# A cross-attention and maxout kernel: a different order of work before and around the arrival of W1

## The chip, the cores and the metric

The kernel runs on one core of a Trainium2 chip. The metric is the device time of one execution in microseconds. Times are shown as the median of several runs; a profile is one further execution, recorded by the hardware profiler.

The core has five engines with instruction streams of their own: PE (TensorE: matmuls and transposes; its weight loads are shown apart, as PEld), DVE (VectorE), ACT (ScalarE), POOL (GpSimd) and SP (SyncE, which here only issues transfers). [...] Transfers between HBM and the on-chip memory run on 16 DMA engines.

## The reference, cut to what matters

```python
# x: (8, 8, 512, 64)  state: (8, 8, 32, 64)   batch, head, rows, width; all f32
scores = x @ state.T / 8;  a = softmax(scores);   xread = a @ state      # (8, 8, 512, 64)
scores2 = state @ x.T / 8; a2 = softmax(scores2); sread = a2 @ x         # (8, 8, 32, 64)
attn = concatenate([xread, sread], axis=2)        # 544 rows for each batch
X = attn.transpose(0, 2, 1, 3).reshape(4352, 512)
h1 = X @ w1; h2 = X @ w2                          # w1, w2: (512, 1024)
out = maximum(h1, h2) @ w_out                     # w_out: (1024, 512), out: (4352, 512)
```

## The kernel before, in words

**Algebra.** Since max(h1, h2) = h2 + relu(h1 - h2), the output is X·(W2·Wout) + relu(X·(W1 - W2))·Wout. The kernel keeps both factors side by side in one bf16 tile `wcat`: columns 0 to 1023 hold W1 - W2, columns 1024 to 1535 hold the product W2·Wout. Rows of X that come from xread are a·state, so the small state is multiplied with `wcat` first: `swt` = state·wcat (`u_sw`, products at L280), and then a·swt gives both h1 - h2 and the first term of the output. The softmax has no maximum subtracted.

**Per batch.** `compact_x` casts x to bf16 in its own layout (`xc`), `cast_x` casts it with a column of ones beside each 64 (`xp`). Transposed x (`xt`) comes from a DMA transpose of `xc` (`d_xt`), for batch 0 from TensorE transposes (`u_xt`). `u_exp` multiplies it with the block-diagonal state `sbd` (16 small matmuls in two groups, L216) and takes exp on ACT. `u_norm` sums, inverts and scales (DVE, and POOL or DVE) into `a`. `u_at` (or `d_at`, by DMA) transposes `a`. `u_sr` reads the state's rows back (32 small matmuls, L239, on `e` and `xp`), and `u_srt` transposes that into `sread_t`, which `moe_sread` uses at the very end. `l1` makes relu(a·swt) in eight column groups f of 128 (two matmuls each, L308, relu in turn on ACT and DVE, into `r`). `l2_open` starts four output banks with the first term (L319), `l2_add` adds r·Wout (L323), `l2_close` copies a bank out.

**Steady state.** For b = 1 to 7 the loop at L531 runs `l1(b)` and `l2(b)` and, in between, the pieces of batch b+1 and b+2 from `fillers`.

**The start.** All loads are issued by SP, on one queue, in the order of the code: state 0, x0 (two parts, even and odd heads), then for each half of W2 that half and two quarters of Wout, then the first half of W1 in two parts (called W1a here), the second half of W1 (W1b), x1, states 1 and 2, x2. `warm_up(n)` issues n matmuls on zeros, which nobody reads. While the weights arrive, PE transposes W2 (`w_t`, L401) and multiplies it with Wout (`w_wo` quarters 0 to 3, L412; `w_wo_out` copies the results into `wcat`). When W1a is in, it is cast (`w1b`), `u_sw(0, 0)` makes the first 512 columns of batch 0's `swt` straight from W1 and W2 (with `sneg`, the negated state), and `u_sw(0, 2)` the last 512. POOL then makes `wcat` columns 0 to 511 (`w_sub(0)`, `w_sub(1)`, L386), DVE makes 512 to 1023 (`w_sub(2)`, `w_sub(3)`) once W1b is in. `l1(0)` runs its first four f, then the second product's parts for these, and later the other four.

**What sets the order.** Every engine executes its instructions in the order of the code: the program is written out by hand, with `tc.manual_schedule()`, and the framework only adds the waits. PSUM has two pools of four banks: `ps` for short-lived results, `acc` for long sums. `xf_t` (f32 x) has two buffers, so x2 is loaded into the one of x0 once its casts are done, and x3 into that of x1.

Of the kernel before, what the change touches and what calls it, by code (L numbers as in the profile page):

```python
# [8 lines left out]
F32 = mybir.dt.float32  # L9
BF16 = mybir.dt.bfloat16  # L10
# [5 lines left out]
def kernel(  # L16
# [42 lines left out]
    def copy(eng, o, i):  # L59
        if eng == "A":  # L60
            nc.scalar.copy(o, i)  # L61
        elif eng == "V":
            nc.vector.tensor_copy(o, i)  # L63
        else:
            nc.gpsimd.tensor_copy(o, i)  # L65
# [11 lines left out]
    def load_x(b, parts=1):  # L77
        xf_t[b] = xio.tile([128, H, NC * D], F32, tag="xf", name="xf")
        for g in range(parts):
            nc.sync.dma_start(out=xf_t[b][:, g::parts, :], in_=x[b, g::parts].rearrange("h (p c) d -> p h (c d)", c=NC))  # L80
# [12 lines left out]
    def load_w(t, w, ch, parts=1):  # L93
        cs = slice(ch * 512, (ch + 1) * 512)
        for k in range(parts):
            i = slice(4 * k // parts, 4 * (k + 1) // parts)
            nc.sync.dma_start(out=t[:, i, cs], in_=w.rearrange("(i p) f -> p i f", p=128)[:, i, cs])  # L97
# [9 lines left out]
        load_wo(2 * ch)  # L107
        load_wo(2 * ch + 1)
    load_w(w1f, moe_w1, 0, 2)
    load_w(w1f, moe_w1, 1)  # L110
    load_x(1)
    load_states(second)
    load_x(2)

    ident = consts.tile([128, 128], BF16)
    warm = consts.tile([128, 512], BF16)
    nc.gpsimd.memset(warm, 0.0)  # L117
    make_identity(nc, ident)
    sbd = consts.tile([128, B, H, 2, Ns], BF16)
# [8 lines left out]
    def warm_up(n):  # L128
        p = bank()
        for k in range(n):  # L130
            nc.tensor.matmul(p, warm[:, 0:128], warm, start=(k == 0), stop=(k == n - 1))  # L131


    s_bf = stage.tile([128, 2 * B, 2, D], BF16)
# [25 lines left out]
    def negate_states():  # L160
        for g in range(2):
            gs = slice(64 * g, 64 * g + 64)
            negate("V", sneg[gs], sbd[gs, 0, g::2, g, :])
# [4 lines left out]
    st = {}  # L168
# [6 lines left out]
    def cast_x(b, parts=(("P", slice(0, 8)),)):  # L175
        new_x(b)
        xp = st[b]["xp"] = xio.tile([128, H, NC, 66], BF16, tag="xp", name="xp")
        nc.gpsimd.memset(xp[:, :, :, 64:65], 1.0)
        for e, hs in parts:
            copy(e, xp[:, hs, :, 0:64], xf_t[b][:, hs].rearrange("p h (c d) -> p h c d", c=NC))  # L180

    def compact_x(b, g, eng="A"):
        new_x(b)
        if g == 0:
            st[b]["xc"] = at.tile([128, H, NC * D], BF16, tag="xc", name="xc")
        copy(eng, st[b]["xc"][:, 4 * g:4 * g + 4], xf_t[b][:, 4 * g:4 * g + 4])


    def d_xt(b):
# [2 lines left out]
    def u_xt(b, g, eng):  # L192
        d = st[b]
        p = bank(BF16)
        for i in range(4):
            for c in range(NC):
                k = 2 * i + c // 2
                nc.tensor.transpose(p[64 * (c % 2):64 * (c % 2) + 64, k * 128:(k + 1) * 128], d["xp"][:, 2 * i + g, c, 0:64], ident)
        copy(eng, d["xt"].rearrange("p (i g u) t -> p g i (u t)", g=2, u=2)[:, g], p.rearrange("p (i w) -> p i w", i=4))

    def u_sc(b, g, mul=nc.gpsimd):
# [28 lines left out]
    def u_sr(b):  # L230

        d = st[b]
        d["sr"] = at.tile([128, 2, D], BF16, tag="sr", name="sr")
        d["rr"] = at.tile([128, 2], F32, tag="rr", name="rr")
        p = bank()
        for g in range(2):
            for c in range(NC):
                for i in range(4):
                    nc.tensor.matmul(p[32 * i:32 * i + 32, g * 65:g * 65 + 65], d["e"][:, g, i, c, :],  # L239
                                     d["xp"][:, 2 * i + g, c, 0:65],  # L240
                                     start=(c == 0 and g == 0), stop=(c == NC - 1 and g == 1))
        pv = p[:, 0:130].rearrange("p (g u) -> p g u", g=2)
        nc.vector.reciprocal(d["rr"], p[:, 64:130:65])
        nc.vector.tensor_mul(d["sr"], pv[:, :, 0:64], d["rr"].unsqueeze(2).to_broadcast([128, 2, D]))
# [173 lines left out]
    def fillers(b):  # L418
        fill = {}

        def put(slot, *units):
            fill.setdefault(slot, []).extend(units)

        n = b + 1
        if n < B:
            put(7, lambda: u_sc(n, 0), lambda: u_sc(n, 1))
            put(8, lambda: u_sr(n))
        if n + 1 < B:
            put(8, lambda: compact_x(n + 1, 0), lambda: compact_x(n + 1, 1))
        if n < B:  # L430
            put(9, lambda: d_at(n))
            put(10, lambda: u_sw(n, 0, 1, 2))
        if n + 1 < B:
            put(10, lambda: d_xt(n + 1))
        if n < B:
            put(11, lambda: u_srt(n))
        return fill

    for b in range(B):
        SW[b] = swt[:, b % 2]  # L440
    warm_up(6)
    cast_states("V", first)
    states(first)
    warm_up(9)
    cast_x(0, (("A", slice(0, 4, 2)), ("V", slice(4, 8, 2)), ("P", slice(1, 4, 2)), ("V", slice(5, 8, 2))))
    u_xt(0, 0, "V")
    warm_up(2)
    u_xt(0, 1, "A")
    u_exp(0, 0)
    warm_up(2)  # L450
    u_exp(0, 1)
    warm_up(3)
    w_cast(w2b, w2f, 0, "PA")
    u_norm(0, 0, nc.vector)
    u_norm(0, 1, nc.vector)
    w_t(0, 0, "A")
    w_t(0, 1, "A")
    u_sr(0)
    wo_cast(0, "P")
    wo_cast(1, "P")  # L460
    warm_up(1)
    for i in range(4):
        w_wo(0, i)
    u_at(0, "V")
    w_cast(w2b, w2f, 1)
    for i in range(4):
        w_wo(1, i)
    w_t(1, 0, "V")
    w_t(1, 1, "A")
    negate_states()  # L470
    wo_cast(2, "P")
    wo_cast(3, "P")
    u_srt(0)
    warm_up(2)
    for i in range(4):
        w_wo(2, i)
    for e, i in (("P", slice(0, 1)), ("A", slice(1, 2)), ("V", slice(2, 3)), ("A", slice(3, 4))):
# [7 lines left out]
    w_sub(0)  # L485
    w_sub(1)
    l1(0, {}, range(0, 4))
    w_sub(2, nc.vector)
    w_sub(3, nc.vector)
    compact_x(1, 0)  # L490
    compact_x(1, 1)
    d_xt(1)
    load_states(rest)
    cast_x(1, (("A", slice(0, 4)), ("A", slice(4, 8))))
    cast_states("P", second)
    compact_x(2, 0, "P")
    compact_x(2, 1, "P")
    d_xt(2)
    load_x(3)
    for c in range(NC):  # L500
        l2_open(0, c)
    l2_add(0, 0, range(0, 4))
    l2_add(0, 1, range(0, 4))
    states(second)
    l2_add(0, 2, range(0, 4))
    u_sw(0, 1)
    l2_add(0, 3, range(0, 4))
    l1(0, {}, range(4, 8))
    u_sw(1, 0)
    u_exp(1, 0)  # L510
    u_exp(1, 1)
    u_norm(1, 0, nc.gpsimd)
    u_norm(1, 1, nc.gpsimd)
    cast_states("P", rest)
# [58 lines left out]
```

The softmax here doesn't subtract the row's maximum and nothing guards it: scores larger than these inputs give would overflow.

## Time and profile before

| what | value |
|---|---|
| median of 8 runs | 150.0 us (149.46 to 151.0) |
| the profiled execution, its own time | 150.05 us |
| its span in the profile | 148.3 us |
| PE busy | 140.2 us, 95% |
| DVE, ACT, POOL busy | 81.2, 75.7, 44.3 us |
| moved by DMA | 29.89 MB, of it 0.16 MB in 10 packets on the queue "instruction" q8 |
| PE busy from 0 to 24.27 us | 20.97 us |
| PE busy from 24.27 to 40.34 us | 15.79 us |
| PE busy from 40.34 to 54.30 us | 13.86 us |

The span is the time from the first to the last instruction; the run's own time is 1.75 us longer. Busy time of PE has modelled ends. A row of a group or of the timeline gives line, engine, operation, output and inputs, shapes and count, and in brackets how long the engine sat idle before and what ended that. In the chain in order of time a row gives start, length, and what the time was spent on. `l1(0)` begins at 24.27 us, `l1(1)` at 40.34 us, `l1(2)` at 54.31 us.

### The profile page before, as it was taken

How to read it: one execution, taken by the hardware profiler on the slowest of the kernel's cores; microseconds unless marked ns; L12 is line 12 of the kernel's file. 1: busy time of each engine (PE TensorE's matmuls, PEld its weight loads, DVE VectorE, ACT ScalarE, POOL GpSimd, SP SyncE). 2: the span in 40 equal slices, each digit the busy share in tenths (PEclk: the TensorE clock that was granted, in tenths of full speed). 3: DMA queues.
4: the chain of work that ended last, by engine and by line, in shares of the span. 5: the costliest groups of instructions: out<-in, count | busy, mean ns of one | idle time of the engine just before them, and what ended most of it. 6: DMA issues, size and time to landing. Idle time of an engine off the chain costs nothing.

```text
span 148.3 us, 3003 instructions
## 1 busy us (share of the span) xinstructions
PE 140.2 (95%) x1228; PEld 67.7 (46%) x1249; DVE 81.2 (55%) x150; ACT 75.7 (51%) x127; POOL 44.3 (30%) x48
## 2 busy tenths in 40 slices
PE   6988989999999999999999999999999999999991
PEld 2455633344454445434543454454445434764460
DVE  5338538848787187535835581668067625721130
ACT  3157348687477177546844692487167036521011
POOL 3145169651949310650072027004100500000000
PEclk9999999999999999999999999999999999999999
DMA  2999999879999949893979497760566031502423
GB/s 74 374 390 386 387 383 339 270 132 212 240 206 380 287 80 288 280 185 102 288 238 186 155 285 197 146 272 13 101 116 283 0 75 46 236 0 70 139 91 131
DMA packets 37982, 29.89 MB, mean 202 GB/s; under 512 B 24912, under 2 KB 33360, under 8 KB 37072
## 3 DMA queue, kind: packets, MB, share of 16 engines
q1 hardware_dynamic: 37824, 29.56, 69.1%
q8 instruction: 10, 0.16, 0.4%
q10 hardware_dynamic: 144, 0.13, 0.3%
q14 instruction: 4, 0.03, 0.1%
HBM read 15.20 MB, written 8.91 MB: 163 GB/s over the span
## 4 chain that ended last, share of the span: by engine, by line
PE 76%; SPq 9%; DMA 9%; issue 2%; POOL 1%; DVE 0%; ACT 0%
PE acc L323 35%; PE ps L308 18%; DMA s_f<-in_state_dram 9%; PE acc L319 8%; SPq L97 4%; PE ps L280 3%; SPq L80 3%; PE ps L367 2%; PE acc L377 2%; PE ps L216 2%; SPq L100 2%; PE ps L239 2%; PE acc L357 1%; PE acc L375 1%; POOL s_bf L65 1%
## 5 line engine op out<-in xcount | busy, mean ns | idle before, releaser
L323 PE MATMUL acc<-wo,r 128*128 128x512 bf16 x238 | 58.3, 379 | 0.5
L323 PEld LDWEIGHTS <-r 128*128 128x128 bf16 x248 | 23.9, 98 | 28.3 <-issue 0.2
L298 DVE TENSOR_SCALAR r<-ps 128x512 bf16<-128x512 f32 x32 | 22.1, 691 | 13.6 <-PE ps L308 13.6
L226 POOL TENSOR_TENSOR a<-e,er 128x512 bf16<-128x512 bf16 x14 | 14.4, 1048 | 50.4 <-ACT e L219 29.7
L308 PE MATMUL ps<-aT,swt 128*128 128x512 bf16 x127 | 29.1, 380 | 0.3 <-DVE swt L63 0.2
L63 DVE COPY ob<-acc 128x512 f32<-128x512 f32 (+1 forms) x17 | 11.1, 655 | 30.2 <-PE acc L323 29.8
L61 ACT COPY ob<-acc 128x512 f32<-128x512 f32 (+1 forms) x16 | 9.2, 572 | 28.9 <-PE acc L323 13.1
L296 ACT ACTIVATE r<-ps 128x512 bf16<-128x512 f32 x32 | 19.2, 601 | 5.9 <-PE ps L308 5.3
L308 PEld LDWEIGHTS <-swt 128*128 128x128 bf16 x128 | 12.1, 98 | 14.9 <-DVE swt L63 0.8
L319 PE MATMUL acc<-swt,aT 128*128 128x512 bf16 x56 | 16.7, 381 | 0.8 <-issue 0.8
L61 ACT CAST swt<-ps 128x512 bf16<-128x512 f32 x18 | 9.9, 587 | 13.1 <-PE ps L280 13.0
L65 POOL CAST xp<-xf 128x2048 bf16<-128x2048 f32 (+1 forms) x7 | 12.2, 1743 | 11.6 <-DMA xf<-in_x_dram 11.6
L61 ACT CAST xc<-xf 128x1024 bf16<-128x1024 f32 x12 | 12.0, 1050 | 1.4 <-DMA xf<-in_x_dram 1.4
L223 DVE TENSOR_REDUCE es<-e 128x16 f32<-128x512 bf16 x16 | 10.6, 660 | 3.6 <-ACT e L219 3.6
L63 DVE CAST swt<-ps 128x512 bf16<-128x512 f32 x18 | 11.6, 678 | 1.1 <-PE ps L280 1.1
L131 PE MATMUL ps<-warm 128*128 128x512 bf16 x24 | 8.7, 498 | 1.3 <-POOL warm L117 1.3
L219 ACT ACTIVATE e<-ps 128x512 bf16<-128x512 f32 x16 | 8.8, 596 | 0.8
L412 PE MATMUL acc<-wo,w2t 128*128 128x512 bf16 x30 | 7.3, 379 | 0.6 <-POOL wo L65 0.5
L319 PEld LDWEIGHTS <-aT 128*128 128x128 bf16 x62 | 4.7, 98 | 6.0 <-issue 2.5
L280 PE MATMUL ps<-wcat,sbd 64*32 64x512 bf16 x136 | 6.2, 383 | 0.0
L216 PEld LDWEIGHTS <-xt 128*128 128x128 bf16 x128 | 4.8, 98 | 2.8 <-ACT xt L61 0.8
L216 PE MATMUL ps<-sbd,xt 128*128 128x64 bf16 x128 | 5.4, 193 | 0.6 <-ACT xt L61 0.6
(74 smaller groups left out, 118.0 us busy)
## 6 DMA issues: line engine op xcount, KB each, us to landing
xf<-in_x_dram SPq DMA_DIRECT2D x7, 1024.0 KB, 7.5
out_dram<-ob SPq DMA_DIRECT2D x7, 1024.0 KB, 5.0
w2f<-in_moe_w_dram SPq DMA_DIRECT2D x2, 1024.0 KB, 9.2
wof<-in_moe_w_out_dram SPq DMA_DIRECT2D x4, 512.0 KB, 11.1
xf<-in_x_dram SPq DMA_DIRECT2D x2, 512.0 KB, 4.6
w1f<-in_moe_w_dram SPq DMA_DIRECT2D x2, 512.0 KB, 13.5
w1f<-in_moe_w_dram SPq DMA_DIRECT2D x1, 1024.0 KB, 14.3
out_dram<-ob SPq DMA_DIRECT2D x3, 256.0 KB, 2.1
```

The lines of the kernel that those rows point to most:

```text
L61: nc.scalar.copy(o, i)
L63: nc.vector.tensor_copy(o, i)
L65: nc.gpsimd.tensor_copy(o, i)
L216: nc.tensor.matmul(p[:, k * 64:k * 64 + 64], d["xt"][:, 4 * i + 2 * g + cp, :], sbd[:, b, 2 * i + g].rearrange("p u n -> p (u n)"), start= ...
L223: nc.vector.tensor_reduce(d["es"][:, g], d["e"][:, g].rearrange("p i c n -> p (i c) n"), axis=mybir.AxisListType.X, op=ALU.add)
L226: mul.tensor_mul(d["a"][:, g].rearrange("p c i n -> p i c n"), d["e"][:, g], d["er"][:, g].rearrange("p (i c) -> p i c", i=4).unsqueeze(3) ...
L280: nc.tensor.matmul(pg[g][32 * i:32 * i + 32, :], sneg[gs, i, :] if k else sbd[gs, b, 2 * i + g, g, :], w[gs, i, ch * 512:(ch + 1) * 512], ...
L296: nc.scalar.activation(out=o, in_=p, func=ACTF.Relu)
L298: nc.vector.tensor_scalar(o, p, scalar1=0.0, scalar2=None, op0=ALU.max)
L308: nc.tensor.matmul(p, SW[b][:, g, f * 128:(f + 1) * 128], AT[b][:, g, :], start=(g == 0), stop=(g == 1))
L319: nc.tensor.matmul(OB[b][1 + c], AT[b][:, g, c * 128:(c + 1) * 128], SW[b][:, g, FF:WC], start=(g == 0), stop=False)
L323: nc.tensor.matmul(OB[b][1 + c], R[b][:, f, c * 128:(c + 1) * 128], wo[:, f, :], start=False, stop=(f == NF - 1))
```

## The change

It reorders the start and makes some of its TensorE work with other instructions:

- x1 and states 1 and 2 are loaded before W1b instead of after it.
- The tile of the warm-ups is f32, 128x256, instead of bf16, 128x512. There are 8 warm-up matmuls (2, 5 and 1) instead of 25 (6, 9, 2, 2, 3, 1 and 2).
- Batch 0's x is transposed from `xc`, 128 columns at a time, in 16 transposes instead of 32 of 64 columns from `xp`. `compact_x` takes its parts as an argument. `xp` of batch 0 is cast later, on ACT, in two copies.
- `negate_states` goes from after `w_t(1)` to before batch 0's casts. The second part of the first half of W2 is cast on DVE instead of ACT.
- `u_sr(0)` and `u_srt(0)` go from before W1 to after `states(second)` and after the second half of `l1(0)`.
- After the first half of `l1(0)`: `w_sub(2)` and `w_sub(3)` come after `states(second)` and `u_sr(0)` on DVE; `states(second)` comes right after `l2_open`, ahead of all `l2_add`; `compact_x(2)` comes later; all four `l2_add(0, c, 0..3)` come before `u_sw(0, 1)`; `u_sw(1, 0)` comes before the second half of `l1(0)`, and `u_exp(1)` inside it, after f = 5.

```diff
     load_w(w1f, moe_w1, 0, 2)
-    load_w(w1f, moe_w1, 1)
     load_x(1)
     load_states(second)
+    load_w(w1f, moe_w1, 1)
     load_x(2)
...
-    warm = consts.tile([128, 512], BF16)
+    warm = consts.tile([128, 256], F32)
...
-            nc.tensor.matmul(p, warm[:, 0:128], warm, start=(k == 0), stop=(k == n - 1))
+            nc.tensor.matmul(p[:, 0:256], warm[:, 0:128], warm, start=(k == 0), stop=(k == n - 1))
...
-    def compact_x(b, g, eng="A"):
+    def compact_x(b, parts=(("A", slice(0, 4)), ("A", slice(4, 8)))):
         new_x(b)
-        if g == 0:
-            st[b]["xc"] = at.tile([128, H, NC * D], BF16, tag="xc", name="xc")
-        copy(eng, st[b]["xc"][:, 4 * g:4 * g + 4], xf_t[b][:, 4 * g:4 * g + 4])
+        xc = st[b]["xc"] = at.tile([128, H, NC * D], BF16, tag="xc", name="xc")
+        for e, hs in parts:
+            copy(e, xc[:, hs], xf_t[b][:, hs])
...
         for i in range(4):
-            for c in range(NC):
-                k = 2 * i + c // 2
-                nc.tensor.transpose(p[64 * (c % 2):64 * (c % 2) + 64, k * 128:(k + 1) * 128], d["xp"][:, 2 * i + g, c, 0:64], ident)
+            for cp in range(2):
+                k = 2 * i + cp
+                nc.tensor.transpose(p[:, k * 128:(k + 1) * 128], d["xc"][:, 2 * i + g, cp * 128:(cp + 1) * 128], ident)
...
-    warm_up(6)
+    warm_up(2)
     cast_states("V", first)
     states(first)
-    warm_up(9)
-    cast_x(0, (("A", slice(0, 4, 2)), ("V", slice(4, 8, 2)), ("P", slice(1, 4, 2)), ("V", slice(5, 8, 2))))
+    warm_up(5)
+    negate_states()
+    compact_x(0, (("A", slice(0, 4, 2)), ("V", slice(4, 8, 2)), ("P", slice(1, 4, 2)), ("V", slice(5, 8, 2))))
     u_xt(0, 0, "V")
-    warm_up(2)
     u_xt(0, 1, "A")
     u_exp(0, 0)
-    warm_up(2)
     u_exp(0, 1)
-    warm_up(3)
-    w_cast(w2b, w2f, 0, "PA")
+    warm_up(1)
+    w_cast(w2b, w2f, 0, "PV")
...
-    u_sr(0)
     wo_cast(0, "P")
     wo_cast(1, "P")
-    warm_up(1)
...
     w_cast(w2b, w2f, 1)
+    cast_x(0, (("A", slice(0, 4)),))
     for i in range(4):
         w_wo(1, i)
     w_t(1, 0, "V")
     w_t(1, 1, "A")
-    negate_states()
+    copy("A", st[0]["xp"][:, 4:8, :, 0:64], xf_t[0][:, 4:8].rearrange("p h (c d) -> p h c d", c=NC))
     wo_cast(2, "P")
     wo_cast(3, "P")
-    u_srt(0)
-    warm_up(2)
     for i in range(4):
         w_wo(2, i)
...
     l1(0, {}, range(0, 4))
-    w_sub(2, nc.vector)
-    w_sub(3, nc.vector)
-    compact_x(1, 0)
-    compact_x(1, 1)
+    compact_x(1)
     d_xt(1)
     load_states(rest)
     cast_x(1, (("A", slice(0, 4)), ("A", slice(4, 8))))
     cast_states("P", second)
-    compact_x(2, 0, "P")
-    compact_x(2, 1, "P")
+    for c in range(NC):
+        l2_open(0, c)
+    states(second)
+    u_sr(0)
+    w_sub(2, nc.vector)
+    w_sub(3, nc.vector)
+    l2_add(0, 0, range(0, 4))
+    l2_add(0, 1, range(0, 4))
+    compact_x(2, (("P", slice(0, 4)), ("P", slice(4, 8))))
     d_xt(2)
     load_x(3)
-    for c in range(NC):
-        l2_open(0, c)
-    l2_add(0, 0, range(0, 4))
-    l2_add(0, 1, range(0, 4))
-    states(second)
     l2_add(0, 2, range(0, 4))
+    l2_add(0, 3, range(0, 4))
     u_sw(0, 1)
-    l2_add(0, 3, range(0, 4))
-    l1(0, {}, range(4, 8))
     u_sw(1, 0)
-    u_exp(1, 0)
-    u_exp(1, 1)
+    l1(0, {5: [lambda: u_exp(1, 0), lambda: u_exp(1, 1)]}, range(4, 8))
+    u_srt(0)
```

## The prediction

> **What bounds the kernel now.** I read the page first: PE is busy 95% of the span. That is an average over a start that waits for weights and a rest that doesn't, so the next view is the chain of work that ended last, in order of time.
>
> ```profile
> PE 140.2 (95%) x1228; PEld 67.7 (46%) x1249; DVE 81.2 (55%) x150; ACT 75.7 (51%) x127; POOL 44.3 (30%) x48
> ...
> q8 instruction: 10, 0.16, 0.4%
> ```
> ```profile
> 14.97 13.33 DMA s_f<-in_state_dram
> 28.35 1.29 POOL s_bf L65
> 29.69 0.40 PE ps L155 x4
> ...
> 40.40 3.57 PE ps L308 x16
> ```
>
> Up to 28.30 us the chain is the load queue: the states of batches 1 and 2 land, POOL casts them, PE transposes them at 29.69. Afterwards it is PE nearly alone; from 40.34 (start of `l1(1)`) each batch takes 13.97 us. The change touches nothing behind that point, so the question is when `l1(1)` starts. The timeline shows what leads there:
>
> ```profile
> 18.12 2.23 POOL L65 CAST wo<-wof 128x1024 bf16<-128x1024 f32 x2 [4.63 <-DMA wof<-in_moe_w_out_dram]
> ...
> 19.21 3.61 PE L412 MATMUL acc<-wo,w2t 128*128 128x512 bf16 x15 [0.54 <-POOL wo L65]
> ...
> 21.99 0.43 DVE L63 CAST w1b<-w1f 128x512 bf16<-128x512 f32 x1 [2.58 <-DMA w1f<-in_moe_w_dram]
> ...
> 22.04 4.91 POOL L386 TENSOR_TENSOR wcat<-w1f,w2f 128x1024 bf16<-128x1024 f32 x2 [0.77 <-DMA w1f<-in_moe_w_dram]
> ...
> 24.27 1.90 PE L308 MATMUL ps<-aT,swt 128*128 128x512 bf16 x8 [0.21 <-DVE swt L63]
> ...
> 30.88 0.41 PE L280 MATMUL ps<-wcat,sbd 64*32 64x512 bf16 x8
> ...
> 31.36 0.69 DVE L63 CAST swt<-ps 128x512 bf16<-128x512 f32 x1 [0.37 <-PE ps L280]
> ```
>
> Before 24.27 every engine waits for a landing: Wout's third quarter (POOL, 18.12), then W1a's second part (DVE, 21.99). From 24.27 PE has next to no gap. So PE work taken out ahead of W1 is worth nothing by itself; PE work put behind 24.27 costs its full time.
>
> But landings are not set by bytes alone. The list of DMA issues, asked in short windows, gives the four Wout quarters in turn, an instruction packet at 15.87, and W1a's second part (issued 9.07):
>
> ```profile
> wof<-in_moe_w_out_dram SPq DMA_DIRECT2D x1, 512.0 KB, 8.1
> ...
> wof<-in_moe_w_out_dram SPq DMA_DIRECT2D x1, 512.0 KB, 8.9
> ...
> wof<-in_moe_w_out_dram SPq DMA_DIRECT2D x1, 512.0 KB, 13.6
> ...
> q8 instruction: 1, 0.02, 68.8%
> ...
> w1f<-in_moe_w_dram SPq DMA_DIRECT2D x1, 512.0 KB, 12.9
> ```
>
> Quarters 0 and 1 (issued 2.85 and 3.40) land at 10.96 and 12.31, 1.35 us apart. W2's second half lands at 15.03; quarter 2 (issued 4.43) should follow at 16.4 and lands at 18.07. Semaphore times show that 15 of 16 DMA engines had delivered it by 16.38 and one came at 18.07; the same engine stays behind to the end (W1a: 15 engines by 20.43, the last 21.97). The step of 1.55 to 1.7 us coincides with that 16 KB packet of PE instructions, 15.87 to 16.97. Without it W1a lands at 20.43.
>
> [...] ten packets of 16 KB for some 2,500 weight loads and matmuls; four of the five packets from the fourth to the eighth began when 256·k minus 62 to 68 of them had started. [...]
>
> **The change, part by part.** (1) *PE ahead of W1.* 25 warm-ups, 16 transposes, `u_sr(0)` and `u_srt(0)` go, 8 f32 warm-ups come. Time: nothing, as said; the cover is the wait for the weights. If that were gone it would be 8.7 us of warm-ups less 8 f32 ones[...]. Count: up to quarter 1's product today 290 instructions (two per matmul), afterwards 148 plus those of the f32 matmuls: 16 if each is one pair, 32 if two, 64 if four. [...] Today that is 12.6 us, and the packet comes 3.2 us later[...]. Afterwards it is the same count: within `w_t(1)`, near 17.0, with 16; at the end of quarter 1's product, near 16.5, with 32; near 15 with 64. With the same 3.2 us the packet starts at 20.2, 19.7 or 18. To spare W1a it must start after 20.4. I take 19.7: W1a lands late, at 21.97, while quarters 2 and 3 land early.
>
> (2) *ACT and DVE ahead of W1.* ACT gets two casts of 1.0 us for `xp`, loses a `w2b` cast (1.04) and `sread_t` (0.27); it sits idle 2.12 and 1.23 us there today. DVE gets a 0.68 us cast before 10.5, where it is idle 1.96. `negate_states` (1.03) delays an x cast that the warm-ups cover until 7. Nothing. SP issues the same 1024 KB and 128 KB in another order; x2 now also waits for ACT's late `xp` casts, near 20, while SP reaches it at 21.
>
> (3) *Start of `l1(0)`.* With W1a at 21.97 DVE's w1b cast, two `wcat` casts and `swt` follow as now: 24.2.
>
> (4) *States earlier in PE's order.* `states(second)` now stands before all `l2_add`. Its cast is on POOL behind both L386 (22.04 to 26.95), a memset (to 27.14) and 1.28 us: 28.42, although the states land by 25.6. PE gets there at 24.2 + 1.73 + 1.73 = 27.7 and stands until 28.47, S. Behind it on PE queue `u_sr(0)`, the 16 `l2_add` and all that follows.
>
> (5) *From S to `u_sw(1, 1)`*, today 29.69 to 35.97, 6.28 us. Afterwards: transposes 0.24; `u_sr(0)` 0.47 with its switch; 16 `l2_add` at 0.216, 3.46; 0.1 for DVE, which ends `sbd` copies, `sr` and two `w_sub` at S + 1.8 + 2.43; then `u_sw(0, 1)` to `l1`, 1.22, as today from 30.88 to 32.10, but filled by 0.34 of `u_sw(1, 0)` where 0.86 of `l2_add` stood; f = 4, 5 0.86; `u_exp(1)` 0.47; f = 6, 7 0.86; `u_srt` 0.06; then `l2_add` needs f = 7, whose relu follows f = 6's on DVE and ACT, ACT having two exps of 0.55 in between: 0.35; four `l2_add` 0.86. Sum 8.95. Of x1's gain (`xt` earlier) nothing is left: PE waited under 0.2 for it.
>
> (6) The rest to `l1(1)` has the same order: 35.97 to 40.34, 4.37.
>
> Sum: 28.47 + 8.95 + 4.37 = 41.79 against 40.34, +1.45 us. The span becomes 149.75, the run 150.05 + 1.45 = 151.5; the profiled run stands 0.05 over the median, so the median as well.
>
> **Rivals.** *The packet comes after 20.4* (not slower). W1a lands at 20.43: L386 runs 20.5 to 25.4; x1 and the states land by 25.6 (the late engine is late for them instead), cast until 26.9, S = 26.95. `l1(0)` starts near 22.8. S + 13.32 = 40.27: 150.0. For it: one pair for an f32 matmul, or a slower fetch, moves the packet by the missing 0.2 to 0.7. Against: 3.2 us is already the longest delay of the ten, counted so; the others are 0.6 to 2.7. It decides at a start of 20.4.
>
> *PE loses its clock.* Today warm-ups start 0.427 us apart until 6.2 us and 0.216 after. With fewer of them between 7 and 12 the products before 16 could run at half speed; quarters 0 and 1 cost 3.4 us more, `l1(0)` starts 1 to 2 us later: 152.5 to 153.5. [...]
>
> *The waits of (4) and (5) are smaller*, with an early W1a: without the 0.8 at S and half of the others, 149.0. For it: POOL's two L386 differ (2.36, 2.60). Against: their chain from W1a to S has no slack anywhere.
>
> *No effect of instruction packets at all*: then 151.5 too.
>
> **How the numbers follow.** Forecast, with the last rival: 0.52, 150.9 to 152.2 by its waits. Packet late: 0.34, 149.5 to 150.8. Clock: 0.08. Smaller waits: 0.06. A measurement of this kernel tells 0.3%, 0.45 us, from no change. Faster: 0.06 and 0.08 out of the second case, 0.14. Same: 0.20 of the second and 0.02 of the first, 0.22. Slower: 0.50, 0.06 and 0.08, 0.64. The range 149.6 to 152.3 leaves out about 0.1 at each end.
>
> **What would show it.** Right: an instruction packet between 17.5 and 20.4, W1a's second cast near 22.0, POOL's state cast ending at 28.4, PE standing 0.7 to 0.8 before L155, a gap of 0.5 between L280 and L308 near 33. Wrong: no such packet before 20.4, and w1b cast at 20.5; or L155 reached by PE later than the cast, which makes POOL harmless; or f32 warm-ups that keep PE beyond 8 us.

## The result, and the profile after

The kernel after takes 150.58 us (median; 150.2 to 150.9), the kernel before, on the same chip, 149.84. The ratio is 1.0044, with a 95% interval from 1.0031 to 1.0057: slower by 0.66 us (0.46 to 0.85). The forecast was 151.5. It had the sign, and the time lies in its range, but it had worked out a loss of 1.45 us, 0.8 us too much. The profiled execution took 150.71 us, its span is 148.9 us.

The page first, its line of busy time and the queue of PE instructions:

```profile
PE 139.5 (94%) x1204; PEld 69.6 (47%) x1224; DVE 81.6 (55%) x151; ACT 76.6 (51%) x128; POOL 44.4 (30%) x48
...
q8 instruction: 9, 0.15, 0.4%
```

PE is 0.7 us less busy in a span that is some 0.7 us longer. Half of the idle time that this adds lies ahead of W1, where the warm-ups went (busy 20.20 of 24.20 us instead of 20.97 of 24.27) and where it costs nothing. One instruction packet fewer came. The chain of work that ended last, in order of time (start, length, what), shows where it is decided now:

```profile
9.13 12.77 DMA w1f<-in_moe_w_dram
...
24.20 1.90 PE ps L308 x8
26.10 1.73 PE acc L319 x8
27.82 0.22 PE ps L155 x4
28.05 0.37 PE ps L239 x32
...
32.39 0.69 DVE swt L63
...
41.07 0.97 PE ps L308 x4
```

Before, the chain was the load queue up to 28.30 us: the states. Now the load of W1a ends in it at 21.90, and from 24.20 it is PE without a step of POOL: L155, the transposes of the states, follows L319 directly. Between there and `l1(1)` the only pieces of another engine are DVE's cast of `swt` at 32.39 and one relu (0.70 us at 34.20). The timeline of each engine has the same places (start, length, engine, line, operation; in brackets the idle time before and what ended it):

```profile
21.97 4.91 POOL L386 TENSOR_TENSOR wcat<-w1f,w2f 128x1024 bf16<-128x1024 f32 x2 [0.76 <-DMA w1f<-in_moe_w_dram]
...
24.20 1.90 PE L308 MATMUL ps<-aT,swt 128*128 128x512 bf16 x8 [0.21 <-DVE swt L63]
...
26.89 0.61 POOL L65 CAST s_bf<-s_f 128x512 bf16<-128x512 f32 x1
...
27.66 0.39 PE L155 MATMUL ps<-ident,s_bf 128*128 128x128 bf16 x4
27.98 0.44 PE L239 MATMUL ps<-xp,e 128*32 128x65 bf16 x32
...
33.13 1.04 PE L308 MATMUL ps<-aT,swt 128*128 128x512 bf16 x4 [0.59 <-DVE swt L63]
...
36.64 0.41 PE L280 MATMUL ps<-wcat,sbd 64*32 64x512 bf16 x8
...
41.00 1.25 PE L308 MATMUL ps<-aT,swt 128*128 128x512 bf16 x5
```

Three things are to be seen. POOL's state cast takes 0.61 us, not the 1.28 of the forecast, and ends at 27.49, before PE wants it: PE starts L155 at 27.66 with no wait. The forecast had named this among its signs of being wrong (L155 reached by PE later than the cast ends). From there everything stands where the forecast put it, 0.8 us earlier: `u_sw(1, 1)` 8.98 us after S (forecast 8.95), `l1(1)` another 4.36 us later (4.37), the gap before f = 4 at 33.13. And `l1(0)` starts at 24.20 as forecast, since W1a is late as before.

The list of DMA issues and queues, asked for 18 to 19.5 us, has the packet of PE instructions that the forecast placed at 19.7, 3.2 us after the start of PE's 180th instruction (that it follows the 180th was the author's assumption); it starts at 18.17:

```profile
q8 instruction: 1, 0.02, 4.7%
```

**Where the 0.66 us come from.** From the start of `l1(0)` to that of `l1(1)` PE takes 16.80 us instead of 16.07; `l1(0)` itself starts 0.07 earlier. Of these 0.73 us, 0.53 are `u_sr(0)` and `u_srt(0)` (0.47 and 0.06), which stand behind W1 now. The rest, 0.20, is a balance of waits: PE now stands 0.59 us before f = 4, to 33.13, and short waits of the kernel before, at L155 and around `u_exp(1)` (L216), are gone. No run takes this balance apart.

### The profile page after: what moved, and what is told of

Read it like the earlier page. It is cut to its first block, busy times and chain, and to the rows that moved or that the text cites. A ratio compares the mean times of both kernels' runs of the same rounds, so it can differ in the third digit from the quotient of the medians.

```text
span 148.9 us, 2957 instructions
## 1 busy us (share of the span) xinstructions
PE 139.5 (94%) x1204; PEld 69.6 (47%) x1224; DVE 81.6 (55%) x151; ACT 76.6 (51%) x128; POOL 44.4 (30%) x48
## 4 chain that ended last, share of the span: by engine, by line
PE 80%; DMA 9%; SPq 5%; DVE 2%; issue 2%; ACT 0%
PE acc L323 36%; PE ps L308 19%; PE acc L319 9%; DMA w1f<-in_moe_w_dram 9%; PE ps L280 3%; SPq L97 2%; PE ps L367 2%; PE acc L377 2%; PE ps L239 2%; SPq L100 2%; PE ps L216 2%; PE acc L357 1%; PE acc L375 1%; DVE swt L63 1%; PE acc L280 1%
## 5 line engine op out<-in xcount | busy, mean ns | idle before, releaser
L308 PE MATMUL ps<-aT,swt 128*128 128x512 bf16 x126 | 29.2, 380 | 1.0 <-DVE swt L63 0.8
L308 PEld LDWEIGHTS <-swt 128*128 128x128 bf16 x128 | 11.9, 98 | 15.5 <-DVE swt L63 1.6
L319 PE MATMUL acc<-swt,aT 128*128 128x512 bf16 x56 | 16.7, 381 | 0.8 <-issue 0.8
L65 POOL CAST xp<-xf 128x2048 bf16<-128x2048 f32 x6 | 11.3, 1890 | 10.6 <-DMA xf<-in_x_dram 10.6
L61 ACT CAST xc<-xf 128x1024 bf16<-128x1024 f32 (+1 forms) x13 | 12.6, 1017 | 3.5 <-DMA xf<-in_x_dram 3.5
L131 PE MATMUL ps<-warm 128*128 128x256 f32 x16 | 7.0, 603 | 1.1 <-POOL warm L117 1.1
L319 PEld LDWEIGHTS <-aT 128*128 128x128 bf16 x62 | 4.7, 98 | 5.9 <-issue 2.5
L280 PE MATMUL ps<-wcat,sbd 64*32 64x512 bf16 x136 | 6.0, 382 | 0.1
L65 POOL CAST xc<-xf 128x1024 bf16<-128x1024 f32 (+1 forms) x3 | 3.3, 1123 | 9.1 <-DMA xf<-in_x_dram 9.1
L216 PEld LDWEIGHTS <-xt 128*128 128x128 bf16 x128 | 4.8, 98 | 2.6 <-DVE xt L63 0.5
```

What stands on the lines that cost most here:

```text
L280: nc.tensor.matmul(pg[g][32 * i:32 * i + 32, :], sneg[gs, i, :] if k else sbd[gs, b, 2 * i + g, g, :], w[gs, i, ch * 512:(ch + 1) * 512], ...
L308: nc.tensor.matmul(p, SW[b][:, g, f * 128:(f + 1) * 128], AT[b][:, g, :], start=(g == 0), stop=(g == 1))
L319: nc.tensor.matmul(OB[b][1 + c], AT[b][:, g, c * 128:(c + 1) * 128], SW[b][:, g, FF:WC], start=(g == 0), stop=False)
```

## The experiments

Three questions: what each part of the change costs, why the cast took half of its price, and what the instruction packet does to the loads. Kernels that ran together share the runs of the kernel before: d1 to d4, d5 to e2, e3 to f3, g2 to g4, and h1 with h2 (its medians are 149.79, 149.76, 149.81, 149.76 and 149.74 us). "W1a" is the landing of its second part on the 15th and on the last of the 16 DMA engines, S the start of L155. These columns are from one profiled execution each, the medians are not. In each of the 18 profiles of this table the execution's own time is 109.70 to 109.74 us more than its `l1(1)`: nothing behind that point makes a difference, as the forecast took it, and what a kernel gains or loses can be read from that column. (d1 is not in the table; its profile is described below.)

| kernel | median, us | ratio to before, 95% | packet | W1a | `l1(0)` | S | `l1(1)` |
|---|---|---|---|---|---|---|---|
| before (first profile) | | | 15.87 | 20.43, 21.97 | 24.27 | 29.69 | 40.34 |
| after (first profile) | | | 18.17 | 20.48, 21.90 | 24.20 | 27.66 | 41.00 |
| d2 | 152.22 | 1.013 to 1.019 | 20.77 | 20.28, 20.42 | 24.99 | 28.45 | 42.52 |
| d3 | 150.34 | 1.0022 to 1.0047 | 18.12 | 20.47, 21.43 | 23.73 | 27.20 | 40.36 |
| d4 | 149.84 | 0.9987 to 1.0015 | 15.77 | 20.54, 21.38 | 23.68 | 28.87 | 39.86 |
| d5 | 150.92 | 1.0058 to 1.0132 | 18.11 | 20.32, 21.57 | 23.87 | 27.63 | 40.98 |
| d6 (after again) | 150.76 | 1.0041 to 1.0080 | 18.17 | 20.41, 22.15 | 24.45 | 27.91 | 41.26 |
| e1 | 150.15 | 1.0018 to 1.0038 | 18.14 | 20.30, 21.62 | 24.01 | 27.47 | 40.34 |
| e2 | 151.30 | 1.0075 to 1.0127 | 18.20 | 20.21, 21.95 | 24.34 | 27.80 | 41.59 |
| e3 | 149.71 | 0.9982 to 1.0003 | 20.76 | 20.33, 20.61 | 23.60 | 27.06 | 39.97 |
| f1 | 149.67 | 0.9985 to 1.0001 | 19.90 | 20.28, 20.43 | 22.99 | 26.45 | 39.74 |
| f2 | 150.85 | 1.0064 to 1.0092 | 19.67 | 20.12, 20.27 | 24.92 | 28.38 | 40.88 |
| f3 (before again) | | | 16.14 | 20.27, 21.79 | 24.37 | 29.79 | 40.43 |
| g2 | 149.57 | 0.9984 to 1.0033 | 19.91 | 20.31, 20.33 | 22.89 | 26.35 | 39.82 |
| g3 | 149.46 | 0.9985 to 1.0023 | 19.65 | 20.25, 21.86 | 24.24 | 27.71 | 40.65 |
| g4 | 149.70 | 0.9988 to 1.0014 | 19.68 | 20.27, 21.85 | 24.24 | 27.70 | 40.14 |
| h1 | 149.51 | 0.9968 to 1.0011 | 21.29 | 20.79, 21.30 | 24.24 | 27.71 | 40.65 |
| h2 | 149.68 | 0.9982 to 1.0015 | 21.05 | 20.67, 20.80 | 23.80 | 27.26 | 40.21 |

### The cast of the states: d1, d4, d5, f3

d1 gives DVE something to do in the kernel after while POOL casts the states:

```diff
     l1(0, {}, range(0, 4))
+    nc.vector.tensor_sub(wcat[:, :, 512:768], w1f[:, :, 0:256], w2f[:, :, 0:256])
     compact_x(1)
```

> The changed kernel plus one two-input subtraction of 128x1024 f32 on DVE right after the first half of l1(0), into a part of wcat that w_sub(2) overwrites later; nothing else differs and no result is used. Theory A: POOL's cast of the states took 0.61 us instead of 1.28 only because DVE no longer ran its own L386 beside it. Then the cast is 1.2 to 1.3 us again, PE stands 0.6 to 0.7 us before L155, and the time is 0.5 to 0.7 us above the changed kernel, 151.1 to 151.3. Theory B: the cast is short because the states have long landed, or because fewer transfers write beside it. Then it stays at 0.6 us and the time at 150.6.

It took 151.9 us (ratio 1.0124 to 1.0188), more than either theory. Its profile can't tell what share is the cast: PE ran at about half clock in it (0.56 on the average), and POOL's cast was over (26.77 to 27.37) long before DVE began the subtraction (33.66). The subtraction alone, 1.22 us, may hold the state copies back on DVE. d5 therefore takes half of it, which fits into DVE's idle time:

```diff
+    nc.vector.tensor_sub(wcat[:, 0:2, 512:768], w1f[:, 0:2, 0:256], w2f[:, 0:2, 0:256])
```

> The kernel after, with one DVE subtraction of 128x512 (half of a w_sub, alone about 0.6 us, its result overwritten later by w_sub(2)) in the stretch 26.8 to 28.1 us in which DVE is idle while POOL casts the states. Theory A, the cast was priced at 1.28 us because in the kernel before DVE's own f32 subtraction ran beside it: the cast takes 0.9 to 1.3 us instead of 0.61, S comes 0.3 to 0.6 us later and the run takes 150.8 to 151.2 us. Theory B, the cast's length has nothing to do with DVE: it stays at 0.61, DVE is free again before the state copies need it, and the time is that of the kernel after, 150.6.

The timeline of d5, DVE's subtraction (L484), POOL's cast, PE's L155:

```profile
26.42 0.68 DVE L484 TENSOR_TENSOR wcat<-w1f,w2f 128x512 bf16<-128x512 f32 x1
...
26.55 1.02 POOL L65 CAST s_bf<-s_f 128x512 bf16<-128x512 f32 x1
...
27.63 0.40 PE L155 MATMUL ps<-ident,s_bf 128*128 128x128 bf16 x4
```

As theory A said, the cast now takes 1.02 us. PE starts L155 3.76 us after `l1(0)` instead of 3.46, so it stands 0.3 us there. The time, 150.92 against 150.76 for the kernel after beside it, is too close to tell; but `l1(1)` follows `l1(0)` by 17.11 instead of 16.81 us, the same 0.30. The size agrees with a POOL that stands until DVE has ended: from 27.10 on, 0.47 us are left, close to the 0.61 of a whole undisturbed cast.

The kernel before, profiled once more (f3), and the kernel before with x1 and the states loaded ahead of W1b and nothing else changed (d4), show both lengths without any added work:

```diff
     load_w(w1f, moe_w1, 0, 2)
-    load_w(w1f, moe_w1, 1)
     load_x(1)
     load_states(second)
+    load_w(w1f, moe_w1, 1)
     load_x(2)
```

> The kernel before once more, for its profile beside the others on the same chip: 149.8 us. Its state cast on POOL takes 1.28 us beside DVE's w_sub again, and l1(1) follows l1(0) by 16.1 us. Were the cast 0.6 us long this time with DVE's w_sub beside it, the theory of two engines in each other's way would be wrong.

> The kernel before with the load order of the change alone: x1 and states 1 and 2 ahead of W1b. PE's order and its instructions are those of before. Theory A: W1b at 28.2 us is early enough for w_sub on DVE (done at 30.7, needed at 30.7), the states no longer wait for their landing: 149.6 to 149.9, no slower than before. Theory B: w_sub, waiting for W1b, holds up DVE's queue with the sbd copies behind it, and u_sw(0, 1) or u_sw(1, 0) starts late: 150.2 to 150.8.

The timeline of f3, with DVE's `w_sub` and POOL's cast of the states:

```profile
26.91 2.35 DVE L386 TENSOR_TENSOR wcat<-w1f,w2f 128x1024 bf16<-128x1024 f32 x2
...
28.35 1.38 POOL L65 CAST s_bf<-s_f 128x512 bf16<-128x512 f32 x1 [1.41 <-DMA s_f<-in_state_dram]
```

And that of d4, where DVE begins only when the cast is over:

```profile
26.36 0.60 POOL L65 CAST s_bf<-s_f 128x512 bf16<-128x512 f32 x1
...
27.73 2.36 DVE L386 TENSOR_TENSOR wcat<-w1f,w2f 128x1024 bf16<-128x1024 f32 x2 [1.42 <-DMA w1f<-in_moe_w_dram]
```

In f3 DVE ends at 29.26 and the cast 0.47 us later, at 29.73; in d5, with 0.55 us beside DVE instead of 0.91, again 0.47 us after DVE. So the cast isn't slowed down in proportion here, it waits for the DVE instruction to end. The other profiles agree: in the 16 in which no DVE subtraction overlaps it, the cast takes 0.60 to 0.63 us. The time of d4, 149.84, is that of the kernel before, as its theory A said: the other order of the loads is worth nothing by itself.

### The parts of the change behind W1: d3, d6, e1

d6 is the kernel after once more, for its profile and its time beside e1 and d5.

> The kernel after once more, beside its variants and on their chip: 150.6 us, 0.7 us over the kernel before. If the late DMA engine's lag differs by chip, W1a's second part lands elsewhere than at 21.9 us and the start of l1(0) moves with it, in both kernels alike.

It took 150.76 us. W1a's last engine comes at 22.15 here, against 21.90 in the first profile: the lag of that engine differs from run to run, on one chip (0.84 us in d4, 1.74 in d6).

e1 puts `u_sr(0)` into PE's idle time ahead of `l1(0)`, with a bank of the pool `acc`:

```diff
     w_sub(1)
+    u_sr(0, "acc")
     l1(0, {}, range(0, 4))
...
     states(second)
-    u_sr(0)
```

> The kernel after with u_sr(0) moved ahead of l1(0), where PE waits about 0.6 us for swt, with a bank of the other pool. Theory A, work put behind the start of l1(0) costs its full length and u_sr(0) is the part of the change that made it slower: 0.47 us less than the kernel after, 150.1 us, u_sw(0,1) at 31.4 and l1(1) at 40.5. Theory B, u_sr(0) only fills time in which PE would wait for DVE's w_sub: at most 0.1 us less, 150.5, with PE standing before u_sw(0,1) instead.

It took 150.15 us, 0.61 less than d6 and still 0.42 over the kernel before (ratio 1.0028), and `l1(1)` follows `l1(0)` by 16.33 instead of 16.81 us. Its timeline on PE:

```profile
23.64 0.44 PE L239 MATMUL acc<-xp,e 128*32 128x65 bf16 x32
24.01 1.90 PE L308 MATMUL ps<-aT,swt 128*128 128x512 bf16 x7
```

L239 ends within the wait for `swt`, and 0.48 us are gone behind it. That is theory A: work moved behind the start of `l1(0)` costs its length, and this one call is more than half of the loss of the change (0.48 of the 0.91 us that d6 lies above the kernel before, 0.48 of 0.66 in the first comparison). What is left, 16.33 against the 16.06 us of f3, is less than the 0.60 us for which PE still stands before f = 4.

d3 tries `u_sr(0)` as cover for that wait instead:

```diff
     states(second)
-    u_sr(0)
...
     u_sw(1, 0)
+    u_sr(0)
     l1(0, {5: [lambda: u_exp(1, 0), lambda: u_exp(1, 1)]}, range(4, 8))
```

> The changed kernel with u_sr(0) after u_sw(1, 0) instead of after states(second), so that it fills part of PE's 0.75 us wait for swt before the second half of l1(0). Theory A: the 0.47 us of u_sr(0) and the wait for swt both stand on PE's path. Then the time falls by 0.4 to 0.5 us to 150.15. Theory B: DVE's w_sub(2), w_sub(3), which end at 31.74, bound u_sw(0, 1) anyway, and PE only waits there instead: 150.5.

150.34 us lies between the two theories, and `l1(1)` follows `l1(0)` by 16.63 instead of 16.80 us: most of the call is still paid. The row shows why the cover is a poor one:

```profile
32.11 0.44 PE L239 MATMUL ps<-xp,e 128*32 128x65 bf16 x32 [0.52 <-ACT swt L61]
```

`u_sr(0)` needs a fifth bank of the pool `ps`, of which the two `u_sw` hold all four, so it waits 0.52 us for the same casts of `swt` that it should cover.

### The instruction packet: d2, e2, e3

d2 issues 20 PE instructions fewer before quarter 2 (3 warm-ups of 512 columns for 8 of 256) and puts `u_at(0)`, 16 more, behind it. The warm-ups' new width is left out of the diff:

```diff
-    warm_up(2)
+    warm_up(1)
...
-    warm_up(5)
+    warm_up(2)
...
-    warm_up(1)
...
-    u_at(0, "V")
...
     for i in range(4):
         w_wo(2, i)
+    u_at(0, "V")
```

> The changed kernel with 36 fewer PE instructions ahead of quarter 2 of W2*Wout: three f32 warm-ups of 512 columns (1 and 2) instead of eight of 256, and u_at(0) after quarter 2 instead of between quarters 0 and 1. Theory A: the 16 KB packet of PE instructions makes one DMA engine late, and its place follows the count. Then it starts later than 18.2 us; if after 20.4, W1a's second part lands at 20.4 instead of 21.9, l1(0) starts near 23.2, and the time is near 149.6; if between, W1a stays at 21.9 and the time at 150.6. Theory B: the late engine has another cause. Then W1a lands at 21.9 wherever the packet is.

Busy time by stretch in d2 (stretch, its length, PE, PEld, DVE, ACT and POOL busy, granted PE clock, DMA share, GB/s):

```profile
7.00:11.30 4.30, 1.32 (x25) 1.09 (x26) 2.64 (x6) 2.11 (x3) 2.46 (x3) 1.00 1.05 385
11.30:14.70 3.40, 2.93 (x19) 2.06 (x21) 2.95 (x4) 1.93 (x2) 2.33 (x3) 0.50 1.06 389
```

Three effects are mixed here. The packet comes at 20.77, and W1a lands at 20.42 on all engines: without the packet ahead of it nothing is late. But PE, busy 1.32 us of 4.3 (2.89 in the kernel after), runs at half clock from 11.3 to 14.7 us and gets to `u_sw(0, 0)` at 22.87, long after W1a. And POOL gets ahead of DVE, in the timeline at W1a's landing:

```profile
20.50 4.85 POOL L386 TENSOR_TENSOR wcat<-w1f,w2f 128x1024 bf16<-128x1024 f32 x2 [0.77 <-DMA w1f<-in_moe_w_dram]
...
21.86 1.27 DVE L63 CAST w1b<-w1f 128x512 bf16<-128x512 f32 x1
```

DVE's cast, 0.43 us elsewhere, ends 0.28 us after the first of POOL's two instructions. The second of DVE's two `w_sub` takes 2.06 us instead of 1.22, begun 0.10 us after a cast of POOL, and `u_sw(0, 1)` waits 0.65 us for it. The run takes 152.2. So the clock can be lost, as the forecast's rival said, though it wasn't in the kernel after; d2 doesn't show what the lost clock alone costs.

e2 is e1 with a cover for f = 4:

```diff
-    states(second)
     w_sub(2, nc.vector)
     w_sub(3, nc.vector)
+    states(second)
...
-    l2_add(0, 3, range(0, 4))
     u_sw(0, 1)
+    l2_add(0, 3, range(0, 4))
     u_sw(1, 0)
```

> The kernel of e1 with two more moves: w_sub(2) and w_sub(3) ahead of the state copies on DVE, and l2_add(0,3) between u_sw(0,1) and u_sw(1,0), so that the 0.75 us in which PE stands before f = 4 for swt are filled. Theory A, both costs of the change are then paid back: 0.9 us less than the kernel after, 149.7 us, which is the kernel before. Theory B, the wait only moves (to the state copies, now behind w_sub, or to the cast of swt behind them): 150.0 to 150.2.

It took 151.30, more than either theory. PE's timeline in e2:

```profile
34.62 0.64 PE L216 MATMUL ps<-sbd,xt 128*128 128x64 bf16 x16 [1.23 <-DMA xt<-xc]
```

The DMA transpose of x1 is late. Its semaphore has 15 engines in by 32.76 and the last at 34.58; the second packet of PE instructions came at 32.37. If the packet did that, one that comes later must free the transpose. e3 tries it: it changes only the shape of the warm-ups of e2, the same PE time in 16 instructions fewer.

```diff
-            nc.tensor.matmul(p[:, 0:256], warm[:, 0:128], warm, ...)
+            nc.tensor.matmul(p.rearrange("p (r n) -> p r n", r=2), warm[:, 0:128],
+                             warm.unsqueeze(1).to_broadcast([128, 2, 256]), ...)
...
-    warm_up(2)
+    warm_up(1)
...
-    warm_up(5)
+    warm_up(2)
```

> The kernel of e2 with its 8 f32 warm-ups of 256 columns made into 4 of 512 (1, 2 and 1): the same PE time and, at four PE instructions each, 16 instructions fewer. Theory A, what spoiled e2 is the second PE instruction packet, which came at 32.37 and made one DMA engine deliver x1's transpose at 34.58 instead of 32.8: with 16 instructions fewer the packet comes after 32.8 us, the transpose is in time, PE doesn't stand before u_exp(1), and the run takes 149.7 to 149.9 us, 1.4 to 1.6 less than e2. The first packet comes 16 instructions later as well, near 19, still ahead of W1a. Theory B, e2 was slow for its own order (the transpose is late by the load of x2 or by the states): 151.3 again.

149.71 us, 1.6 less than e2, as theory A said. The second packet comes at 33.93, x1's transpose is in by 32.66, and L216 starts at 32.96 with no wait. The first packet moved farther than expected, from 18.20 to 20.76, so that W1a is on time here too, 20.61. The gain of e3 over e2 is thus not the transpose alone: `l1(0)` starts 0.74 us earlier, `l1(1)` 1.62. Nor is the packet shown to be what made the transpose late. In e1, f2, g2, g3, g4, h1 and h2 too the second packet starts 0.26 to 0.60 us before x1's transpose is complete (in e1 at 32.20, with all in by 32.56), and there no engine is late. Why it was in e2 stays open.

### What a punctual W1a is worth: f1, f2, g2, g3, g4, h1, h2

f1 is e3 with `u_at(0)` in the gap after `w_t(1)`:

```diff
-    u_at(0, "V")
     w_cast(w2b, w2f, 1)
...
     w_t(1, 1, "A")
+    u_at(0, "V")
```

f2 is e3 with `u_at(0)` behind quarter 2, as in d2.

> The kernel of e3 with u_at(0) after w_t(1), in the 0.34 us in which PE waits for w2t, instead of before quarter 1's product. Theory A, the start of l1(0) hangs on W1a: quarters 2 and 3 are multiplied 0.4 us earlier and PE waits for W1a as much longer; 149.6 to 149.8 us, at most 0.1 less than e3. Theory B, PE is the bound from 13 to 22 us: l1(0) and all after it start 0.3 to 0.4 us earlier, 149.3 to 149.4 us.

> The kernel of e3 with u_at(0) after quarter 2's product: 180 PE instructions are then started only near 18, so that the first packet is the latest that this order allows. Theory A, a packet after 20.4 us leaves W1a's second part on time at 20.4 on all engines, but PE gets to u_sw(0,0) no earlier than 21.9, so the start of l1(0) stays near 24.1: an early W1a by itself is worth nothing; 149.7 to 149.9 us. Theory B, W1a alone sets the start: l1(0) at 23 and 148.7 to 149.0 us. If the packet comes before 20.4, W1a is late as before and neither is tried.

In f1 all of the start runs 1.38 us ahead of f3: `l1(0)` at 22.99. The time, 149.67, is only 0.14 below before; between the two profiles `l1(1)` differs by 0.69 us, but f3's run (150.15) lies 0.34 over the median of the kernel before and f1's (149.48) 0.19 under its own. PE's timeline in f1:

```profile
22.99 1.90 PE L308 MATMUL ps<-aT,swt 128*128 128x512 bf16 x7
...
30.21 0.41 PE L280 MATMUL ps<-wcat,sbd 64*32 64x512 bf16 x8 [0.79 <-DVE wcat L386]
...
39.74 2.55 PE L308 MATMUL ps<-aT,swt 128*128 128x512 bf16 x11
```

PE stands 0.79 us for DVE's `w_sub`, which waits for W1b: with the packet at 19.90 one engine is late for W1b (26.68 on 15 engines, 27.78 on the last), as it is in the kernel after (26.79, 28.23). The early start meets the next load of the queue, and more than half of its 1.38 us is given back there.

f2 came out at 150.85, though W1a is on time (20.27). Its timeline:

```profile
20.34 4.85 POOL L386 TENSOR_TENSOR wcat<-w1f,w2f 128x1024 bf16<-128x1024 f32 x2 [0.78 <-DMA w1f<-in_moe_w_dram]
...
20.71 2.27 DVE L63 CAST w1b<-w1f 128x512 bf16<-128x512 f32 x1
```

DVE was still copying `aT` when W1a landed, POOL began first, and DVE's cast of 0.43 us took 2.27: it ended 0.28 us after the first of POOL's two instructions (20.35 to 22.70). That looks like the exclusion of the states' cast with the roles changed, and the cast is on PE's path (`u_sw(0, 0)`). Neither theory for f2 had it. The other profiles bear it out. In 17 of the 19 DVE's cast began some 0.05 us ahead of POOL: it took 0.43 us, and POOL's first instruction 2.59 or 2.60, its second 2.34 to 2.37. In f2 and d2 POOL was first: its first instruction took 2.35 and 2.36, DVE's cast ended 0.28 us after it, and POOL's second took 2.54 and 2.53. g4 is f2 with `aT` copied by ACT:

```diff
-    u_at(0, "V")
+    u_at(0, "A")
```

> The kernel of f2 with batch 0's transposed a copied by ACT instead of DVE. In f2 W1a's second part was on time (20.27), DVE came to its w1b cast at 20.71, 0.37 us after POOL had begun w_sub(0), and the cast took 2.27 us instead of 0.43. Theory A, the two engines exclude each other for a whole instruction and the first to start wins: DVE is now free when W1a lands, starts its cast no later than POOL its w_sub, the cast takes 0.43 to 0.5 us, l1(0) starts 0.9 to 1.1 us earlier than in f2 (23.8 to 24.0 instead of 24.92) and the run takes 149.8 to 150.1 us. Theory B, the cast was long for another reason (its source had just landed, or two engines read W1 at once): it stays over 1 us and the time at 150.8.

149.70 us. The timeline of g4:

```profile
21.87 0.43 DVE L63 CAST w1b<-w1f 128x512 bf16<-128x512 f32 x1 [4.21 <-DMA w1f<-in_moe_w_dram]
...
21.92 4.93 POOL L386 TENSOR_TENSOR wcat<-w1f,w2f 128x1024 bf16<-128x1024 f32 x2 [2.37 <-DMA w1f<-in_moe_w_dram]
```

The cast takes 0.43 us. As a test it is weaker than meant: in the profile the packet (19.68) came ahead of W1a's end and W1a was late (21.85), so DVE, which was done with `aT` at 20.79 in f2, would have been free in time without ACT's help.

g2 is f1 with the state copies ahead of `w_sub` on DVE again and `u_sw(1, 0)` ahead of `u_sw(0, 1)`, to fill the 0.79 us; g3 is g2 without the first warm-up.

```diff
+    states(second)
     w_sub(2, nc.vector)
     w_sub(3, nc.vector)
-    states(second)
...
+    u_sw(1, 0)
     u_sw(0, 1)
     l2_add(0, 3, range(0, 4))
-    u_sw(1, 0)
```

> The kernel of f1, in which l1(0) starts 1.4 us earlier than in the kernel before but PE then stands 0.79 us for w_sub, with the state copies ahead of w_sub on DVE again (DVE is idle from 25.6 to 27.8) and u_sw(1,0) ahead of u_sw(0,1). Theory A, the early start was given back because w_sub waits for W1b's last engine near 27.8: u_sw(1,0) fills 0.35 us of that wait and the run takes 149.3 to 149.4 us, 0.3 less than f1. Theory B, it was given back elsewhere (PSUM banks, or the casts of swt, of which DVE gets one more behind w_sub): 149.6 to 149.8 as f1. If the second instruction packet (32.53 in f1, with x1's transpose landed at 32.42) comes before the transpose, PE stands up to 1.4 us more and it shows as a late engine.

> The kernel of g2 without its first warm-up, so 4 PE instructions fewer ahead of everything. Theory A, only the count moves: both packets come 4 instructions (0.2 to 0.4 us) later, x1's transpose is farther from the second, and the time is that of g2 or, where g2's transpose was hit, 149.3 to 149.4. Theory B, the clock needs that warm-up: PE is at full speed only after 8 us and the products of batch 0 come late; 149.6 to 150.5.

They took 149.57 and 149.46 us. PE still stands for `w_sub` in g2, since W1b's last engine came at 28.18 in the profiled run:

```profile
30.61 0.41 PE L280 MATMUL ps<-wcat,sbd 64*32 64x512 bf16 x8 [0.94 <-DVE wcat L386]
```

The times fall into two groups with nothing between: g2 has 8 of 14 at 149.22 to 149.60 and 6 at 150.36 to 150.91, g3 14 of 22 at 149.12 to 149.81 and 8 at 150.33 to 150.90. The two profiles are one of each kind: g2 (149.54) with the packet at 19.91 and W1a at 20.33, g3 (150.37) with the packet at 19.65 and W1a at 21.86. h1 is g2 with `u_at(0)` back before quarter 1's product, which moves the packet away from there; h2 is h1 without the first warm-up.

```diff
     for i in range(4):
         w_wo(0, i)
+    u_at(0, "V")
...
     w_t(1, 1, "A")
-    u_at(0, "V")
```

> The kernel of g2 with u_at(0) back before quarter 1's product, as in e3: w_t(1) ends 0.45 us later, and with it PE's 180th instruction. Theory A, the two groups of times of g2 and g3 (near 149.35 and near 150.6) are a race of the first packet (19.65 to 19.91) with the end of W1a on one engine, and e3's packet at 20.76 is clear of it: all runs lie near 149.4, none above 150.2, the median 149.35 to 149.5, and W1a's last engine lands by 20.7. Theory B, the groups have another cause (the second packet and x1's transpose, or the exclusion of DVE and POOL at 20.35): two groups again.

> The kernel of h1 without its first warm-up, 4 PE instructions fewer. Theory A: the packet comes still later, 20.9 to 21.2, and the time is h1's, 149.35 to 149.5, in one group. Theory B: two groups, or a loss of 0.3 us or more because PE reaches its full clock 2 us later.

With packets at 21.29 and 21.05, h1 has 9 of 11 runs at 149.22 to 149.93 and h2 12 of 13 at 149.34 to 149.92; 150.39, 151.01 and 150.96 remain. So the upper group nearly goes, and the race with the packet is the likely cause of most of it; it isn't all, since h1's profile is the run of 150.39, in which 15 engines too deliver 0.5 us later than in e3. None of e3, f1, g2, g3, g4, h1 and h2 is shown to be faster than the kernel before: the medians are 149.46 to 149.71 against 149.74 to 149.81, and every interval holds 1.

## Why the forecast had the sign right and the size wrong

**Step 4 failed: POOL's cast.** The step put the states' cast at 1.28 us, taken from the row of the kernel before (28.35, 1.29 in the chain), and from it came S = 28.47 and a PE that stands 0.8 us. The cast takes 0.61 where DVE leaves POOL alone, as it does at 26.89 in the kernel after, because the change itself moved `w_sub` behind it on DVE. In the kernel before the timelines of POOL and DVE have

```profile
20.66 0.61 POOL L65 CAST w1b<-w1f 128x512 bf16<-128x512 f32 x1 [0.32 <-DMA w1f<-in_moe_w_dram]
...
26.81 2.35 DVE L386 TENSOR_TENSOR wcat<-w1f,w2f 128x1024 bf16<-128x1024 f32 x2
...
28.35 1.28 POOL L65 CAST s_bf<-s_f 128x512 bf16<-128x512 f32 x1 [1.22 <-DMA s_f<-in_state_dram]
```

The 1.28 was 0.8 us of waiting for DVE's L386 (27.96 to 29.17) and 0.47 of casting. S was 27.66, PE's own arrival. With that in its place the sum gives 27.66 + 8.95 + 4.37 = 40.98 for `l1(1)`, 150.05 + 0.64 = 150.7; measured were 41.00 and, in the profiled run, 150.71. The whole error of 0.8 us is in this one step: 0.67 in the cast's length, and 0.25 in its start, which was put at the end of POOL's memset (27.14) and came at 26.89, beside it. They add up to more than 0.8 because PE itself arrives only at 27.66.

The profile before held both warnings, in these rows: POOL's cast of `w1b`, the same 128x512 from f32 to bf16, takes 0.61 us, and L386 of DVE runs to 29.17, over the first 0.8 us of the slow cast. The forecast even named POOL's two L386 (2.36 and 2.60) as unequal and didn't ask why: in g4, where the first runs from 21.93 to 24.53, it begins while DVE casts `w1b` (21.87 to 22.30).

**Step 1 came out right by luck.** The packet was put 3.2 us after the 180th instruction; it came at 18.17, when 212 had started, 1.34 us after the 180th (16.83). So the delay was 1.34 us and not 3.2. Which instruction a packet belongs to was the author's assumption; no trace shows it. Since both 18.17 and 19.7 are ahead of W1a's end on that engine, W1a was late as forecast (21.90 for 21.97). Nor does the count hold from kernel to kernel: counted in the same way (twice the weight loads), the third to sixth packet of the kernel after began some 50 instructions past 256·k, not 62 to 68 short of it. The 8 f32 warm-ups are 16 weight loads and 16 matmuls in the profile, two pairs each, the middle one of the three cases; those of the group of five start 0.85 us apart after the first (4.35, 5.20, 6.05 and 6.91 us). The threshold was put at 20.4; the runs put it near 19.7: packets at 19.67 (f2), 19.90 and 19.91 left W1a on time, those at 19.65 and 19.68 (g3, g4) did not. In every profile with the packet at 19.65 or before W1a's last engine is 0.84 us or more behind the 15th, and in every one with it at 19.90 or later 0.51 or less, so "no effect of packets" has fallen. f1 shows besides that a punctual W1a doesn't bring the 1.5 us by which the last engine had been late.

**Step 2, nothing ahead of W1,** holds: `l1(0)` starts at 24.20 for 24.2. **Step 3** the same.

**Steps 5 and 6** hold within 0.03 us: 8.98 and 4.36. e1 gives `u_sr(0)` by itself 0.48 us for the 0.47 of step 5; the gap of 0.5 between L280 and L308 near 33 is there (0.59, to 33.13).

**The rivals.** "The packet comes after 20.4" was to bring 150.0 with S at 26.95. f1, with another order behind W1, is the nearest to it: S is 26.45, and it shows a path that the rival didn't have, W1b's landing, which takes 0.79 us of the gain. "PE loses its clock" didn't happen (granted 1.00 in each stretch from 7.0 to 24.2 us); d2, where it does, takes 152.2, beside the 152.5 that the rival named at the least, but the clock isn't its only loss. "The waits are smaller" had 0.06 and is the one that names what happened, no wait at S, though it put that together with an early W1a and at 149.0. The forecast held against it that the chain from W1a to S has no slack anywhere; the slack was in the cast.

## What to carry to other kernels

The duration of a row is a price only if the engine did nothing but that work in it: look for the same shape elsewhere in the timeline, and where two rows of one shape differ, find what ran beside the longer one before moving it. For these casts and subtractions on DVE and POOL that was the other of the two, and the engine that started first decided, so an order turned 0.43 us into 2.27. In this kernel, work that went out of the stretch that waits for loads brought nothing (`l1(0)` at 24.20 for 24.27), and work that went into the stretch behind cost its whole length: `u_sr(0)` alone was 0.48 us of this loss of 0.66.

## What the runs showed of the hardware

- Where DVE's subtraction met POOL's cast of the states, and POOL's subtraction DVE's cast of `w1b`, the one that began second was longer by about the rest of the other's instruction. POOL's cast of 128x512 took 0.60 to 0.63 us in 16 profiles and 1.28, 1.38 and 1.02 in the three in which a DVE subtraction of two SBUF inputs was under way; it then ended 0.47 us after that subtraction. With POOL's subtraction first, DVE's cast of 0.43 us took 1.27 (d2) and 2.27 (f2) and ended 0.28 us after it.
- With the first PE instruction packet, of 16 KB, came one DMA engine of 16 that was late for the loads still queued: W1a's last engine is 0.84 to 1.74 us behind the 15th in the ten profiles of the table with the packet at 19.65 us or before, and 0.02 to 0.51 in the six with it at 19.90 or later; between them it was 0.15 behind with 19.67 (f2) and 1.58 with 19.68 (g4). In the kernel after it is 1.43 us behind for W1a, x1 and the states and 1.44 for W1b. In f1, with the packet at 19.90, W1b is late in its place (by 1.10). For x1's transpose the runs don't agree: late in e2, on time in seven kernels with the packet just as near.
- The number of PE instructions moves the packet: e3 does the same as e2 in 16 instructions less, and the first packet came 2.6 us later. But the 180th instruction started only 0.87 us later (17.50 for 16.63); the rest of the move isn't explained, so a packet's time can't be forecast from the count alone.
- PE dropped to half clock (0.50 granted, 11.3 to 14.7 us), for 3.4 us, after a stretch in which it was busy 31% of 4.3 us (d2). In e3, with one warm-up more in the same stretch, it was busy 51% and stayed at full clock (1.0 in the mean of the execution, 0.989 in d2), as in the kernel after with 67%. Where the limit lies isn't shown: e3 kept full clock through 41% of 3.4 us (6.5 to 9.9 us), and d2 lost it after 37% (7.9 to 11.3).
